# Expert 0's first 256 rows multiplied while the last batch is routed

## The chip, the cores and the metric

One Trainium2 chip, of which the kernel uses one core. The metric is the time of one execution in microseconds on the device. The kernel before was run three times: 780.51, 781.54 and 781.69 us, median 781.54. Less is better.

## The reference

```python
# q, k, v, alpha: (4, 8, 768, 48); 3072 tokens of 384 features, 8 experts of width 1024
for t in range(S):
    state = alpha[:, :, t, :, None] * state + np.einsum('bhd,bhe->bhde', k[:, :, t], v[:, :, t])
    y[:, :, t] = np.einsum('bhd,bhde->bhe', q[:, :, t], state)
...
expert_idx = np.argmax(logits, axis=1)            # logits: normed x times normed embeddings, by tau
gate_w = probs[np.arange(N), expert_idx]
for e in range(E):
    mask = expert_idx == e
    h = np.maximum(x[mask] @ w1[e], 0.0)
    out[mask] = gate_w[mask, None] * (h @ w2[e])
...
h = x @ w_in                                      # 384 -> 2048 -> 384 for every token
g = np.maximum(0.01 * h, h)
return (g @ w_out).astype(np.float32)
```

A gated linear attention over four batches gives 3072 tokens. Each token goes to the expert with the largest score (top 1); the expert's two layers are applied to it, and a dense pair of layers to the result. In the reference's inputs expert 0 has 309 tokens in the first three batches and 418 in all four; the largest expert has 426.

## The kernel before

The work has three stages. In the first, attention runs in 16 units (4 batches of 4 pairs of heads), and each finished batch is routed: scores, largest score, rank of the token within its expert, and then six indirect DMAs from GpSimd (`scatter`, L595) write the batch's 768 rows to `bucket`, a table in DRAM with 3072 rows for each expert. The rows carry the scale, the gate and the token's number behind the 384 features. The routing of a batch runs inside the next batch's attention; that of the last batch has nothing beside it.

In the second stage (from L800) the eight experts follow one another. Of each, exactly 432 rows (`CAP`) are computed, more than any expert has here: what is beyond its tokens was zeroed earlier by `zero_rows`, and a loop at the end (L1067) takes what is past 432, which is empty here. Every number is kept as a pair of f16 values (high and low), so a product takes three: high by high, high by low, low by high. The first layer (`up`) has 8 groups (f) of 3 x 3 products of 432 columns, the second (`down`) 3 groups (d) of 8 x 3; together 144 products. Expert 0's rows are fetched in four blocks, scaled on VectorE, turned on TensorE (`first_rows`, L853); the other experts' rows are scaled to f16 pairs on ScalarE and VectorE and turned by DMA (`block`, L875). Meanwhile the next expert's weights are fetched in 8 pieces of 384 KB (L892), into five stage buffers, and split into f16 pairs on ScalarE and VectorE (L897, L898), and a part of the last layers' 64-bit weights is converted on the way (`double`, L907).

In the third stage the dense pair of layers runs over blocks of 512 tokens.

In the first two stages the order of the instructions on each engine comes from a planner (`Plan`, L44): every operation is added with an engine, a cost, what it reads and writes, and a due time `at`. `order` takes at each step the operation that can start first, and among those within 0.15 us of it the one with the smallest `at`. The second plan's DMA is modelled at 230 KB/us. Each engine then executes in that order; on SyncE (SP), which issues most DMAs, it is also the order of the transfers' issue. In the first plan, fillers (`keep_busy`, L335) are put where TensorE would be idle. A tile of a later stage that takes the place of an earlier stage's memory waits for all that used it: for SBUF this includes the scatters, which read the batch's rows. PSUM has a pool of its own.

Between the plans stand the sum of the counts (L711 to L721), which gives `n_e`, and 56 fillers (L714). In the second plan `START` (L820) and `begin(e)` set the due times; `pieces_of(e)` lists expert e+1's pieces and the 64-bit pieces by due time, and L987 puts the first four ahead of expert 0's rows.

## Time and profile before

| | us |
|---|---|
| median of three runs | 781.54 |
| the profiled execution's own time | 780.79 |
| its span, first to last instruction | 779.2 |
| TensorE busy | 757.4 (97%) |
| VectorE busy | 452.4 (58%) |
| ScalarE busy | 341.0 (44%) |
| GpSimd busy | 98.9 (13%) |

TensorE's busy time counts the fillers as well: 172 of them in the trace, 53.2 us. A group of rows below is read as: start and length in us, engine, line, operation, out<-in, shapes, count, and in brackets the idle time of the engine before it with what ended it. PE is TensorE's product, PEld its load of weights, DVE VectorE, ACT ScalarE, POOL GpSimd, and SPq the issue of a DMA on SyncE. Start times count from the first instruction of the span.

### The profile page before, as it was taken

To read this page: it belongs to the slowest core of one execution; us is meant where nothing else is said; L and a number is where in the kernel's file an instruction comes from. 1 tells how busy PE (TensorE), PEld (TensorE's weight loads), DVE (VectorE), ACT (ScalarE), POOL (GpSimd) and SP (SyncE) were. 2 spreads that over 40 slices of the span, in tenths; PEclk is the share of its full clock that TensorE was granted. 3 is DMA by queue.
4 is the path that set the end of the run, shared out by engine and by line. 5 is a ranking of instruction groups with operands and counts; after the bars stand their busy time and mean duration, and the time that the engine had idled before them with its cause. 6 is when DMAs were issued, how large, how long until landed. Compare 5 with 4: busy or idle time off the path is not lost.

```text
span 779.2 us, 12948 instructions
## 1 busy us (share of the span) xinstructions
PE 757.4 (97%) x5109; PEld 426.8 (55%) x5109; DVE 452.4 (58%) x776; ACT 341.0 (44%) x673; POOL 98.9 (13%) x108
## 2 busy tenths in 40 slices
PE   8999999988999999999999999999999999999995
PEld 4777767644555555555544654554554564465462
DVE  8989999747688788878866126116306404503600
ACT  2343636416576676757635125215205404403500
POOL 6122624321010000000000110010010010010011
PEclk9999999999999999999999999999999999999998
DMA  8984945228998998787100000000000000000000
GB/s 301 349 257 133 294 140 191 93 96 208 198 226 218 225 247 171 212 229 222 42 3 1 20 21 1 11 31 0 11 21 11 1 31 11 1 21 21 1 21 23
DMA packets 58466, 84.08 MB, mean 108 GB/s; under 512 B 26648, under 2 KB 37664, under 8 KB 58400
## 3 DMA queue, kind: packets, MB, share of 16 engines
q1 hardware_dynamic: 54752, 73.66, 34.7%
q0 software_dynamic: 3648, 9.53, 3.2%
q8 instruction: 42, 0.69, 0.4%
q14 instruction: 24, 0.20, 0.1%
HBM read 66.80 MB, written 11.73 MB: 101 GB/s over the span
## 4 chain that ended last, share of the span: by engine, by line
issue 46%; PE 39%; DVE 5%; POOL 4%; DMA 3%; ACT 1%; SPq 0%; POOLq 0%; ACTq 0%
PE ps L965 4%; PE ps L964 4%; PE ps L963 4%; PE ps L940 4%; PE ps L939 4%; PE ps L938 4%; POOL out L797 3%; PE psc L396 2%; PE py L447 2%; PE py L415 2%; PE pfill L336 2%; DMA v<-in_v 1%; DVE rc L369 1%; PE ptr L475 1%; DVE am L401 1%
## 5 line engine op out<-in xcount | busy, mean ns | idle before, releaser
L780 DVE SCALAR_TENSOR_TENSOR g<-ps,r 128x512 f32<-128x512 f32 x96 | 65.7, 684 | 150.2 <-ACT r L779 150.2
L792 PE MATMUL ps<-woh,gh 128*128 128x384 f16 x384 | 125.2, 326 | 0.0
L793 PE MATMUL ps<-wol,gh 128*128 128x384 f16 x384 | 125.2, 326 | 0.0
L794 PE MATMUL ps<-woh,gl 128*128 128x384 f16 x384 | 125.2, 326 | 0.0
L774 PE MATMUL ps<-x2h,wih 128*128 128x512 f16 x288 | 109.1, 379 | 1.4 <-DVE x2l L970 1.4
L775 PE MATMUL ps<-x2l,wih 128*128 128x512 f16 x288 | 109.2, 379 | 0.0
L776 PE MATMUL ps<-x2h,wil 128*128 128x512 f16 x288 | 109.2, 379 | 0.0
L784 DVE TENSOR_TENSOR gl<-g,gh 128x512 f16<-128x512 f32 x96 | 66.4, 692 | 65.4 <-ACT gh L783 65.4
L783 ACT ACTIVATE gh<-g 128x512 f16<-128x512 f32 x96 | 60.4, 630 | 82.7 <-DVE g L780 82.6
L796 ACT ACTIVATE osb<-ps,ms 128x384 f32<-128x384 f32 x24 | 14.0, 582 | 159.3 <-PE ps L794 159.3
L797 POOL DMA_INDIRECT out<-osb,tki x24 | 23.7, 987 | 352.1 <-ACT osb L796 345.2
L938 PE MATMUL ps<-xt,w1h 128*128 128x432 f16 x192 | 66.4, 346 | 0.0
L939 PE MATMUL ps<-xt,w1h 128*128 128x432 f16 x192 | 66.4, 346 | 0.0
L940 PE MATMUL ps<-xt,w1l 128*128 128x432 f16 x192 | 66.4, 346 | 0.0
L963 PE MATMUL ps<-hh,w2h 128*128 128x432 f16 x192 | 66.4, 346 | 0.0
L964 PE MATMUL ps<-hl,w2h 128*128 128x432 f16 x192 | 66.4, 346 | 0.0
L965 PE MATMUL ps<-hh,w2l 128*128 128x432 f16 x192 | 66.4, 346 | 0.0
L779 ACT ACTIVATE r<-ps 128x512 f32<-128x512 f32 x96 | 56.0, 583 | 10.8 <-PE ps L776 10.8
L336 PE MATMUL pfill<-busy,ones 128*128 128x512 f16 x172 | 53.2, 411 | 2.1 <-POOL busy L189 2.1
L793 PEld LDWEIGHTS <-gh 128*128 128x128 f16 x384 | 37.6, 98 | 25.1
L792 PEld LDWEIGHTS <-gh 128*128 128x128 f16 x384 | 37.6, 98 | 25.1
L794 PEld LDWEIGHTS <-gl 128*128 128x128 f16 x384 | 37.6, 98 | 24.8
(198 smaller groups left out, 1131.6 us busy)
## 6 DMA issues: line engine op xcount, KB each, us to landing
wstage<-in_w SPq DMA_DIRECT2D x64, 384.0 KB, 5.7
a<-in_aT SPq DMA_DIRECT2D x16, 387.5 KB, 4.4
k<-in_kT SPq DMA_DIRECT2D x16, 384.0 KB, 6.2
q<-in_qT SPq DMA_DIRECT2D x16, 384.0 KB, 6.6
wstage<-in_w_in SPq DMA_DIRECT2D x16, 384.0 KB, 5.7
wstage<-in_w_out SPq DMA_DIRECT2D x16, 384.0 KB, 3.5
v<-in_v SPq DMA_DIRECT2D x8, 576.0 KB, 7.9
xg<-bucket SPq DMA_DIRECT2D x7, 582.0 KB, 7.2
```

Of the source, the lines that this page charges most:

```text
L774: nc.tensor.matmul(ps, wih[:, k, fs], xh[:, k], start=k == 0, stop=False)
L775: nc.tensor.matmul(ps, wih[:, k, fs], xl[:, k], start=False, stop=False)
L776: nc.tensor.matmul(ps, wil[:, k, fs], xh[:, k], start=False, stop=k == KD - 1)
L792: nc.tensor.matmul(ps, ghs[f][:, ts], woh[:, f], start=f == 0, stop=False)
L793: nc.tensor.matmul(ps, ghs[f][:, ts], wol[:, f], start=False, stop=False)
L794: nc.tensor.matmul(ps, gls[f][:, ts], woh[:, f], start=False, stop=f == NF2 - 1)
L938: nc.tensor.matmul(ps, w1h[:, f, k], xt[:, k], start=k == 0, stop=False)
L939: nc.tensor.matmul(ps, w1h[:, f, k], xt[:, KD + k], start=False, stop=False)
L940: nc.tensor.matmul(ps, w1l[:, f, k], xt[:, k], start=False, stop=k == KD - 1)
L963: nc.tensor.matmul(ps, w2h[:, f, cols], hh, start=f == 0, stop=False)
L964: nc.tensor.matmul(ps, w2h[:, f, cols], hl, start=False, stop=False)
L965: nc.tensor.matmul(ps, w2l[:, f, cols], hh, start=False, stop=f == NF1 - 1)
```

## The change

Expert 0 is split by rows: its first 256 (`E0`) and the other 176. When the third batch's rows are in the bucket, the first 256 rows of expert 0 are fetched within the first plan (`early_rows`), scaled on ScalarE, turned on TensorE and kept as f16 pairs (`xte`). The second plan has both layers of expert 0 for these 256 columns ahead of everything else, and for the other 176 columns after expert 0's last two blocks of rows. The hidden values (`hid`) and `xte` lie in a pool that is made ahead of the routing stage (`keep`); `xte` shares its place with the sign buffers of the 64-bit pieces, and the hidden values' tiles are used again in the last layers. The 56 fillers between the plans and the twelve of `first_rows` are gone. `START` is 5.5 and not 20. Six and not four pieces of weights stand ahead of the gathers; expert 1's rows are fetched in blocks and have an early due time. The token numbers and gates of expert 0 are copied from DRAM to DRAM. If expert 0 had fewer than 256 tokens in three batches (`few`), its first two blocks would be computed again in the loop for leftovers.

```diff
+E0 = 2 * P
...
+    seen, few = (const.tile([P, 1], F32, name=n) for n in ("seen", "few"))
+    keep = ctx.enter_context(tc.tile_pool(name="keep", bufs=1))
+    hid = [[keep.tile([P, BLK], F16, name=f"h{x}{f}") for f in range(NF1)] for x in "hl"]
+    shared = keep.tile([P, 2 * W64], F32, name="shared")
+    xte = shared.bitcast(F16).rearrange("p (k t) -> p k t", k=2 * KD)
...
+            if b == B - 2:
+                small(V, lambda: nc.vector.tensor_copy(seen, cnt[:, 0:1]), ["cnt"], ["seen"])
...
+        def early_rows():
+
+            u = (NU - 3) % 3
+            rows = (ta[u][:, :AUG], tq[u][:, :AUG])
+            scaled = (ta[u][:, AUG:AUG + D], tk[u][:, :D])
+            for n in range(E0 // P):
+                ts = slice(n * P, (n + 1) * P)
+                hi, lo = xte[:, :KD, ts], xte[:, KD:, ts]
+                held = ("a", "q")[n], u
+
+                def fetch(n=n, ts=ts):
+                    nc.sync.dma_start(rows[n], bucket[ts])
+
+                def turn(n=n):
+                    for k in range(KD):
+                        nc.tensor.transpose(ptr[n][:, k], scaled[n][:, k * P:(k + 1) * P], ident)
+
+                plan.add(Q_, 0.45, fetch, [("bucket", B - 2, c) for c in range(NC)], [held], size=(P * AUG * 4, 2.5))
+                plan.add(S_, 0.62, lambda n=n: nc.scalar.activation(scaled[n], rows[n][:, :D], AF.Copy, scale=rows[n][:, D:D + 1]), [held], [("early", n)] + [("k", u)] * n)
+                plan.add(T_, 0.45, turn, [("early", n)], [("tr", n)], pe=[f"t{n}"], flow=KD * P)
+                plan.add(S_, 0.47, lambda n=n, hi=hi: nc.scalar.activation(hi, ptr[n][:, :KD], AF.Copy), [("tr", n)], [("xte", n)], ps=[f"t{n}"])
+                plan.add(V, 0.56, lambda n=n, hi=hi, lo=lo: nc.vector.scalar_tensor_tensor(lo, ptr[n][:, :KD], 1.0, hi, op0=ALU.mult, op1=ALU.subtract),
+                         [("tr", n), ("xte", n)], [("xtl", n)], ps=[f"t{n}"])
...
-            z0 = 2 * P
+            z0 = 0 if e == 0 else 2 * P
 
             def go():
-                nc.sync.dma_start(bucket[e * NT + z0:e * NT + z0 + P], zero)
-                nc.sync.dma_start(bucket[e * NT + z0 + P:e * NT + CAP], zero[:CAP - z0 - P])
+                for o in range(z0, CAP, P):
+                    nc.sync.dma_start(bucket[e * NT + o:e * NT + min(o + P, CAP)], zero[:min(P, CAP - o)])
...
+            plan.at = NU + 1.7
+            early_rows()
...
-            nc.vector.tensor_copy(tc16, cnt)
-            tot = pkv[:, 0:E]
+            nc.vector.tensor_copy(tc16[:, :E], cnt)
+            nc.vector.tensor_copy(tc16[:, E:], seen)
+            tot = pkv[:, 0:E + 1]
             nc.tensor.matmul(tot, ones16, tc16, start=True, stop=True)
-            for _ in range(56):
-                keep_busy("f")
-            nc.vector.tensor_tensor(n_e, tot, row0, op=ALU.subtract)
+            nc.vector.tensor_scalar(few, tot[:, E:], float(E0), None, op0=ALU.is_lt)
+            nc.vector.tensor_tensor(n_e, tot[:, :E], row0, op=ALU.subtract)
...
-        START, TURN = 20.0, 26.4
+        START, TURN = 5.5, 26.4
...
-            if e == 0:
-                for n in range(NB):
-                    plan.add(Q_, 0.45, lambda n=n: block(n), ["bucket"], [("xg", 0), ("row", n)], size=(P * AUG * 4, 2.5), at=0.0)
+            if e < 2:
+                for n in range(0 if e else E0 // P, NB):
+                    plan.add(Q_, 0.45, lambda n=n: block(n), ["bucket"], [("xg", e), ("row", e, n)], size=(P * AUG * 4, 2.5), at=float(e))
             else:
-                plan.add(Q_, 0.9, most, ["bucket"], [("xg", e % 2)] + ([("row", n) for n in range(NB)] if e == 2 else []), size=CAP * AUG * 4, at=begin(e - 2) + 8 if e > 1 else 20.0)
+                plan.add(Q_, 0.9, most, ["bucket"], [("xg", e % 2)] + [("row", e % 2, n) for n in range(NB)], size=CAP * AUG * 4, at=begin(e - 2) + 8,
+                         after=[("xt", 1, NB - 1, 0)] if e == 2 else ())
...
+                if e == 0:
+                    nc.gpsimd.dma_start(meta[:CAP], bucket[:CAP, D + 1:D + 3])
+                    return
...
-                for _ in range(6 if n == NB - 1 else 2):
-                    nc.tensor.matmul(ps2[3], ones16, busy[:, :CAP], start=True, stop=True)
...
-            at = begin(e - 1) + 1.0 + 4.0 * n
-            plan.add(S_, 0.62, lambda: nc.scalar.activation(xs[:, 0], x, AF.Copy, scale=r), [("xg", e % 2)], [("xs", g, 0)], at=at)
+            at = begin(e - 1) + 1.0 + 4.0 * n if e > 1 else n - 15.0
...
-        def up(e, f):
-            xt, (w1h, w1l), ps = xts[e % 2], shaped(sets[e % 2])[:2], ps1[f % 4]
-            hh, hl = hid[0][f], hid[1][f]
-            at = begin(e) + 1.65 * f - 12.0
+        def step(n):
+
+            return max(0.1, n * 0.1828 / CAP)
+
+        def up(e, f, xt, at, cols, early=False):
+            (w1h, w1l), n = shaped(sets[e % 2])[:2], cols.stop - cols.start
+            ps, hh, hl = ps1[f % 4][:, :n], hid[0][f][:, cols], hid[1][f][:, cols]
 
             def go():
                 for k in range(KD):
@@ -939,9 +977,11 @@
                     nc.tensor.matmul(ps, w1h[:, f, k], xt[:, KD + k], start=False, stop=False)
                     nc.tensor.matmul(ps, w1l[:, f, k], xt[:, k], start=False, stop=k == KD - 1)
 
-            plan.add(T_, 1.65, go, [("w", e % 2, 0, f // 2, i) for i in range(2)] + [("xt", e % 2, n, i) for n in range(NB) for i in range(2)], [("ps1", f % 4)], at=at)
-            plan.add(S_, 0.52, lambda: nc.scalar.activation(hh, ps, AF.Relu), [("ps1", f % 4)], [("h", f, 0)], at=at)
-            plan.add(V, 0.605, lambda: nc.vector.scalar_tensor_tensor(hl, ps, 0.0, hh, op0=ALU.max, op1=ALU.subtract), [("ps1", f % 4), ("h", f, 0)], [("h", f, 1)], at=at)
+            rows = [("sg", i) for i in range(2)] if early else [("xt", e % 2, b, i) for b in range(cols.start // P, NB) for i in range(2)]
+            key = ("h", f, early)
+            plan.add(T_, 9 * step(n), go, [("w", e % 2, 0, f // 2, i) for i in range(2)] + rows, [("ps1", f % 4)], at=at)
+            plan.add(S_, 0.16 + n / 1200, lambda: nc.scalar.activation(hh, ps, AF.Relu), [("ps1", f % 4)], [(*key, 0)], at=at)
+            plan.add(V, 0.155 + n / 960, lambda: nc.vector.scalar_tensor_tensor(hl, ps, 0.0, hh, op0=ALU.max, op1=ALU.subtract), [("ps1", f % 4), (*key, 0)], [(*key, 1)], at=at)
...
+            for f in range(NF1):
+                up(0, f, xte, f - 40.0, slice(0, E0), True)
+            for d in range(KD):
+                down(0, d, d - 30.0, slice(0, E0), True)
             mine = pieces_of(0)
-            add(mine[:4])
+            add(mine[:6])
             gather(0)
             gather(1)
-            add(mine[4:])
-            for n in range(NB):
+            add(mine[6:])
+            for n in range(E0 // P, NB):
                 first_rows(n)
...
+                cols = slice(0 if e else E0, CAP)
                 for f in range(NF1):
-                    up(e, f)
+                    up(e, f, xts[e % 2][:, :, cols], begin(e) + 1.65 * f - 12.0, cols)
...
+            E1 = E + 1
+            spare = shared[:, :2 * OVB * E1].rearrange("p (m e) -> p m e", e=E1)
...
```

`down` is split in the same manner as `up`; expert 0's results go to a fixed place (columns 0 to 431), so the reading of its offset falls away. The block that computes the leftovers' list (L1019) has nine entries instead of eight and some eight small VectorE instructions more. Expert 0's rows are zeroed from row 0.

## Rows read from the trace of the kernel before

**Rows 1.** The page's head: the span of the profiled execution.
```profile
span 779.2 us, 12948 instructions
```

**Rows 2.** Busy time by stage: stretch, its length, engines, granted clock, DMA share, GB/s.
```profile
core 0: us, PE busy (x) PEld busy (x) DVE busy (x) ACT busy (x) POOL busy (x), PEclk, DMA share, GB/s
...
173.00:178.00 5.00, 4.09 (x19) 1.67 (x17) 3.68 (x6) 3.33 (x6) 0.00 (x0) 1.00 0.82 225
178.00:184.10 6.10, 3.88 (x25) 2.40 (x26) 4.57 (x11) 2.27 (x5) 0.83 (x1) 1.00 0.98 340
184.10:210.40 26.30, 26.30 (x146) 14.11 (x145) 19.11 (x35) 16.67 (x31) 3.15 (x5) 1.00 0.81 161
210.40:236.80 26.40, 26.40 (x146) 14.13 (x145) 20.71 (x35) 16.76 (x31) 2.07 (x3) 1.00 1.01 242
```

**Rows 3.** Time line of PE, from routing's end into expert 0's second layer.
```profile
163.14 0.17 PE L713 MATMUL pkv<-c,ones 128*128 128x8 f16 x1 [1.43 <-DVE c L711]
...
165.63 11.46 PE L336 MATMUL pfill<-busy,ones 128*128 128x512 f16 x48
179.78 0.52 PE L860 MATMUL ps<-ident,xs 128*128 128x128 f32 x3 [2.69 <-issue]
...
184.06 0.35 PE L938 MATMUL ps<-xt,w1h 128*128 128x432 f16 x1
...
197.20 0.35 PE L963 MATMUL ps<-hh,w2h 128*128 128x432 f16 x1
```

**Rows 4.** Loads of weights: time line in routing; by line (ns min/median/max) for the experts.
```profile
161.38 0.20 PEld L575 LDWEIGHTS <-ones 128*128 128x128 f16 x5 [0.82 <-issue]
...
L938 PEld LDWEIGHTS <-w1h x192: 97/98/98, 183.9 to 380.4; 128*128 128x128 f16 x192
```

**Rows 5.** Time lines of ACT, DVE, POOL and SP in the same stretch.
```profile
161.23 0.24 ACT L582 ACTIVATE ex<-lg 128x48 f32<-128x48 f32 x1 [1.61 <-DVE lg L581]
172.64 0.84 ACT L897 ACTIVATE w1h<-wstage 128x768 f16<-128x768 f32 x1 [11.17 <-DMA bucket<-xb,slot]
...
163.34 0.17 DVE L716 TENSOR_TENSOR n_e<-pkv,row 128x8 f32<-128x8 f32 x1 [0.26 <-PE pkv L713]
173.52 0.96 DVE L898 SCALAR_TENSOR_TENSOR w1l<-wstage,w1h 128x768 f16<-128x768 f32 x1 [8.44 <-ACT w1h L897]
178.87 1.03 DVE L864 TENSOR_SCALAR xs<-xg 128x384 f32<-128x384 f32 x2
...
163.30 0.97 POOL L596 DMA_INDIRECT bucket<-xb,slot  x1 [7.83 <-issue]
169.67 0.96 POOL L596 DMA_INDIRECT bucket<-xb,slot  x1 [0.30 <-issue]
...
172.57 1.75 SPq L829 DMA_DIRECT2D xg<-bucket  x4
```

**Rows 6.** Landing: third batch's scatters; expert 0's gathers; fetches of 175 to 180.
```profile
L596 POOL DMA_INDIRECT bucket<-xb,slot x6: 965/967/1172, 147.9 to 154.5; - x6
DMA to landing us min/median/max: 2.6/2.7/5.0
...
DMA to landing us min/median/max: 2.5/3.2/3.9
...
DMA to landing us min/median/max: 5.9/6.6/7.7
```

**Rows 7.** Busy time and granted clock in two short stretches (columns as in rows 2).
```profile
165.00:167.00 2.00, 2.00 (x6) 0.69 (x5) 0.08 (x1) 0.00 (x0) 1.52 (x2) 0.50 0.45 164
177.00:179.70 2.70, 0.10 (x1) 0.00 (x0) 2.70 (x5) 0.77 (x2) 0.83 (x1) 1.00 0.99 290
```

**Rows 8.** Last conversions for experts 1 and 4 (DVE); expert 4's second layer begins (PE).
```profile
210.19 0.96 DVE L898 SCALAR_TENSOR_TENSOR w2l<-wstage,w2h 128x768 f16<-128x768 f32 x1 [2.34 <-ACT w2h L897]
299.74 0.94 DVE L898 SCALAR_TENSOR_TENSOR w2l<-wstage,w2h 128x768 f16<-128x768 f32 x1
...
302.32 0.35 PE L963 MATMUL ps<-hh,w2h 128*128 128x432 f16 x1
```

More of the change, by code (lines that the diff above doesn't have):

```diff
@@ L536, in part_squares @@
             x, w = txb[b % 3][:, :, 2 * h * HD:2 * (h + n) * HD], late[:, :, :2 * n * HD]
-            small(S_, lambda: nc.scalar.activation(w, x, AF.Square), [("xb", b % 3, u, g) for u in range(h, h + n) for g in range(2)], ["late"], 0.2 + 0.48 * n)
+            small(S_, lambda: nc.scalar.activation(w, x, AF.Square), [("xb", b % 3, u, g) for u in range(h, h + n) for g in range(2)], ["late", ("junk", 0), ("junk", 1)], 0.2 + 0.48 * n)
             small(V, lambda: nc.vector.tensor_reduce(tsm[b % 2][:, row], w, AX.X, ALU.add), ["late"], [("part", h)], 0.1 + 0.6 * n)
@@ L780, in second_in @@
             nc.vector.scalar_tensor_tensor(g, ps, 2.0 ** -6, r, op0=ALU.mult, op1=ALU.max)
-            gh = gp.tile([P, n], F16, name=f"gh{f}")
-            gl = gp.tile([P, n], F16, name=f"gl{f}")
+            gh, gl = (hid[i][f][:, :n] if f < NF1 else gp.tile([P, n], F16, name=f"g{i}{f}") for i in range(2))
             nc.scalar.activation(gh, g, AF.Copy)
@@ L967, in down @@
             for f in range(NF1):
-                plan.add(T_, 0.55, lambda f=f: go(f), [("w", e % 2, 1, f // 2, i) for i in range(2)] + [("h", f, i) for i in range(2)], [("ps2", b)], at=at + 0.55 * f)
-            plan.add(S_, 0.52, lambda: nc.scalar.activation(x2h[:, d, ds(offset[0], CAP)], ps, AF.Copy, scale=2.0 ** -8), [("ps2", b), ("place", 0)], [("x2", e, d)], at=at)
-            plan.add(V, 0.605, lambda: nc.vector.scalar_tensor_tensor(x2l[:, d, ds(offset[1], CAP)], ps, 2.0 ** -8, x2h[:, d, ds(offset[1], CAP)], op0=ALU.mult, op1=ALU.subtract),
-                     [("ps2", b), ("x2", e, d), ("place", 1)], [("x2l", e, d)], at=at)
+                plan.add(T_, 3 * step(n), lambda f=f: go(f), [("w", e % 2, 1, f // 2, i) for i in range(2)] + [("h", f, early, i) for i in range(2)], [("ps2", b)], at=at + 0.05 * f)
@@ new lines, in place @@
+            def place(i):
+                return cols if e == 0 else ds(offset[i], CAP)
+            where = [] if e == 0 else [("place", i) for i in range(2)]
+            plan.add(S_, 0.16 + n / 1200, lambda: nc.scalar.activation(x2h[:, d, place(0)], ps, AF.Copy, scale=2.0 ** -8), [("ps2", b)] + where[:1], [("x2", e, d)], at=at)
+            plan.add(V, 0.155 + n / 960, lambda: nc.vector.scalar_tensor_tensor(x2l[:, d, place(1)], ps, 2.0 ** -8, x2h[:, d, place(1)], op0=ALU.mult, op1=ALU.subtract),
+                     [("ps2", b), ("x2", e, d)] + where[1:], [("x2l", e, d)], at=at)
```

92 lines of the change are left out of this document (49 added, 43 removed).

## The prediction

> **What bounds the kernel now.** I read the page's head first (the span, [rows 1]), then the time line of TensorE around the end of routing, then the time lines of the other engines in the same stretch, then the busy time by stage, and last the conversions of the weights. TensorE is busy nearly everywhere, so busy time says little; what matters is which of its work is the kernel's. From the last product of routing at 163.14 to the first product of expert 0 at 184.06 it computes nothing that is kept: 57 fillers, of which one row has 48, then a gap of 2.69 us, then turns of rows with more fillers [rows 3]. These 20.9 us are a chain on other engines: scores of the last batch, six scatters on POOL from 163.30, the last at 169.67, their landing, the gathers on SP at 172.57, and behind ACT's first conversion (172.64, after 11.17 us of waiting for the scatters) a queue of conversions, until VectorE scales expert 0's first rows at 178.87 [rows 5]. Behind the chain stand eight experts of even length. Expert 0's first layer is 72 products of 432 columns in 184.06 to 197.20 [rows 3], 0.1825 us each. An expert has 144, so 26.3 us, and TensorE is full in that stage [rows 2]. Only two things shorten the kernel here: an earlier first product of the rest, or less work behind it. The change aims at the second.
>
> **What is removed and added on TensorE.** Expert 0's 144 products of 432 columns (26.3 us) become 144 of 256 columns ahead of the release and 144 of 176 behind it. At a granted clock of 1.00 (2.4 GHz) 432 columns are 180.0 ns of the 182.5, so I price a product at columns/2.4 GHz + 2.5 ns: 109.2 ns for 256, 15.7 us for the early block. For 176 that gives 75.8 ns, 10.9 us, if nothing but columns counts. The other end is the load of the weights: each product has one, 97 to 98 ns long [rows 4]; if loads of different weights ran one after the other the rest would take 144 x 97.5 = 14.0 us. But in the routing's small products five such loads of 128x128 f16 fit into 0.20 us, so they start about 25 ns apart and overlap [rows 4]. I take 80 ns, 11.5 us, near the low end, and keep both.
>
> The row says that a load does not hold up the next product for its length. The Trainium skill ("TensorE: Matmul & The Clock Gate", section "LDWEIGHTS (loading the stationary operand)") speaks against the change here: it prices a load at columns/1.2 in ns, 107 ns for 128, and by that the rest would be 15.4 us, 3.9 us more than I take; the same page's "Back-to-back issue gap" has about 81 ns for a sustained pair at 128 columns, which would make it 11.7 us at least. No run before shows distinct weights with so few columns.
>
> **When the early block runs.** It needs the scatters of the third batch, its own rows, and PSUM. The third batch's last scatter starts at 154.5 and these land in 2.6 to 5.0 us [rows 6], so SP can fetch at 157.3 to 159.5; two fetches of 128 rows land 2.5 to 3.9 us later [rows 6], by about 161 to 163.4. They read the bucket that the last batch's scatters write, so POOL's scatter, at 163.30 [rows 5], waits for them: nothing at the near end, 0.1 us at the far one; I take nothing. The plan's ready times put the early scaling on ACT behind the last batch's Exp (161.23 [rows 5]), and the early low halves on VectorE behind its routing chain; so nothing of routing is queued behind a fetch except that scatter. Scaling, turning and splitting two blocks cost by the planner 0.62 + 0.45 + 0.47 + 0.56 us, two of them overlapped: done at about 164.3. The counts wait behind them on VectorE (n_e moves from 163.34 to about 165.2), but nobody needs n_e before the experts. The first early product waits for n_e, since that is the last read of the routing's PSUM: about 165.4. The clock is at 0.50 (1.2 GHz) in 165 to 167 [rows 7], after the gap that ends with the sum of the counts [rows 3]; I let that stand for 2 us of early block, +1.0 us. So the block ends at 165.4 + 15.7 + 1.0 = 182.1, under the wait. Its evacuations are hidden except in one place: ACT has the first conversion of expert 1's weights between the sixth and the seventh Relu by the planner's times, and that conversion waits for the release (172.64). The sixth group's Relu is due at about 172.4, so this costs nothing at half clock, up to 1 us without; both ends stay under the wait.
>
> **When the rest starts.** Before the gathers SP now has six fetches instead of four. The early fetch holds the first four back from the 140s to about 159, which hides behind the release. The fifth waits for the release, and the sixth takes stage buffer 0, freed by ACT's first conversion and VectorE's part of it: 172.64 + 0.84 + 0.96 = 174.5. So the gathers leave at about 175.0 instead of 172.57 and land, behind a fetch, in 2.5 to 6.6 us [rows 6], at 178 to 181. Two more pieces (some 3 us of VectorE) stand ahead of the scaling, but two blocks instead of four follow it. Before, the way from the first scaling to the first product was 184.06 - 178.87 = 5.2 us for four blocks. With scaling at 180 and 4 us for two blocks and the conversions between, I get 184.5; bounds 183 (conversions hide) and 186 (the sixth piece lands late and ACT waits for it). So the start stays where it was, within the bounds.
>
> **The sum up to expert 1.** 184.5 + 11.5 = 196.0, against 184.06 + 26.3 = 210.4: 14.4 us. This is where it can be given back: expert 1's rows and every later weight are wanted 14.4 us earlier.
>
> **The supply.** Expert 1's last piece of weights is converted at 210.19 + 0.96 = 211.2 [rows 8], wanted at 210.4 + 13.1 + 3.3 (the seventh of eight steps of its second layer) = 226.8: 15.6 us to spare. Expert 4's is ready at 299.74 + 0.94 = 300.7, wanted at 302.32 + 3.3 = 305.6 [rows 8]: 4.9 us. Three experts' pieces took 89.5 us, where TensorE takes 78.9. With demand 14.4 us earlier, 9.5 us must be found or TensorE waits. In 173 to 210.4 the DMA engines were idle for 0.18 x 5 + 0.02 x 6.1 + 0.19 x 26.3 = 6.0 us [rows 2]; two gather blocks fewer, and two fetches some 3 us earlier, give 3 to 4 more. After 210.4 hardly anything is left (share 1.01). So 9 to 10 us against 9.5: I take 1.5 us of waiting, spread over experts 1 to 4, ends 0 and 9.5.
>
> **Small edits.** Zeroing 256 more rows of expert 0 is 0.4 MB in the attention stage; put_meta(0) goes from DRAM to DRAM and frees the row buffer earlier; one copy (seen) in batch 2: nothing, between engines that wait for others there. Some eight more small VectorE operations stand ahead of the last layer's evacuations, 0.17 us each like n_e [rows 5], 1.4 us; the last layer has four PSUM banks of work in hand: 0 to 1.4, I take 0.2. In the reference's inputs expert 0 has 309 tokens in the first three batches and 418 in all, no expert over 426: the early rows are full, and the loop for leftovers stays empty.
>
> Sum: -14.4 + 1.5 + 0.2 = -12.7 us against the profiled execution, 780.79 with a span of 779.2 [rows 1]: 768.1. The median of the three runs is 781.54, 0.75 higher, so I say 769.0. Best within the bounds: 183, 10.9, no waiting: 16.5 us, 764.8 to 765.0. Worst: 186, 14.0, 3 us of waiting: 7.4 us, 774.
>
> **Rivals.** (1) Weight loads set the pace of the narrow products: 14.0 us instead of 11.5, and some 0.5 us less of waiting for supply: 771. For it: loads 97 ns long; against it: starts 25 ns apart [rows 4]. 0.15. (2) The supply cannot be pulled forward, since conversions stand in fixed orders between evacuations and DMA is full: only the 4.9 us that expert 4 has to spare are gained, 776.6. For it: share 1.01 in 210 to 237 [rows 2]; against it: 0.81 before that, and that the orders move with TensorE. 0.15. (3) The change doesn't do what it says: the early products wait for the release of the routing stage's memory, as ACT's conversion does (172.64): the block ends at 172.6 + 15.7 = 188.3, the rest starts at 188.8, 4.3 us of the gain are lost and about 1 of waiting saved: 772.3. Against it: they write only PSUM and tiles made outside that stage. 0.07. (4) Slower: without the 57 fillers and the twelve of the turns the clock stays at 1.2 GHz over both narrow blocks. Then the early block ends at 165.4 + 31.2 = 196.6 and the rest takes 144 x 147 = 21.2 us: 218.2 against 210.4, +7.8 us, 789. It decides once some 29 us of this stretch run at half, since each costs half a microsecond of 14.4. Against it: the 2.7 us without products at 177 to 179.7 left the clock at 1.00 [rows 7], and the early block is dense. 0.05.
>
> **How the numbers follow.** Forecast 0.57, rivals 0.15, 0.15, 0.07, 0.05, and 0.01 for a net near nothing. The range 764.5 to 776 holds the forecast's bounds, rivals 1 and 3 and the near half of 2; left out are the rest of 2, 4 and the forecast's tail, under 0.2. A change under 0.2% (1.6 us) could not be told from none. Faster 0.94, same 0.01, slower 0.05.
>
> **What would show it.** In the trace after: products of 256 columns from about 165 and before the last scatter lands; their spacing 109 ns; the rest at 183 to 186; the spacing of the 176-column products, 76 to 98 ns, decides rival 1; expert 1 at 195 to 200; TensorE's waits between there and 300, none before, sum to 0 to 3 us (rival 2: 9); granted clock 0.50 for 2 us or for 29. The forecast is wrong if the gathers leave later than 176, if TensorE waits more than 4 us for weights, or if the scatters move from 163.3.

## The result and the profile after

The changed kernel takes 771.76 us (median of four runs, 769.78 to 773.2), the kernel before 781.56 beside it: ratio 0.9876, 95% interval 0.9852 to 0.99, 9.8 us less. The forecast was 769.0 with a range of 764.5 to 776, so the time is inside, 2.8 us above the forecast. The profiled execution has a span of 769.7 against 779.2 [rows 1], 9.5 us less; the forecast's sum was 12.7. What follows finds the 3.2 us between these.

TensorE's busy time by stage in the trace after (stretch, its length, busy time and products, granted clock, share of the DMA engines, GB/s); these answer to [rows 2, 7]:

```profile
166.20:183.60 17.40, 17.37 (x144) 0.90 0.51 160
183.60:186.05 2.45, 1.05 (x9) 1.00 0.99 325
186.05:197.20 11.15, 11.14 (x144) 1.00 1.00 219
197.20:381.90 184.70, 184.33 (x1009) 1.00 0.84 206
381.90:384.76 2.86, 0.17 (x1) 1.00 0.00 0
384.76:388.20 3.44, 3.44 (x9) 0.50 0.00 0
```

The first row is the early block, 144 products with part of them at half clock. The second is the step to the rest of expert 0: turns and a wait. The third is the rest, the fourth experts 1 to 7. The last two are new: an idle step ahead of the third stage, and behind it nine products at half clock. The same two stretches of the kernel before:

```profile
394.30:395.84 1.54, 0.17 (x2) 1.00 0.11 2
395.84:399.30 3.46, 3.46 (x17) 1.00 0.45 9
```

There the step is 1.3 us shorter, and 17 products pass in the time of nine.

TensorE's time line in the trace after, around the early block, the rest and expert 1; it answers to [rows 3]:

```profile
162.35 0.18 PE L580 MATMUL psc<-oh,before 128*128 128x48 f16 x1 [0.55 <-DVE oh L576]
...
165.65 0.17 PE L749 MATMUL pkv<-c,ones 128*128 128x9 f16 x1 [1.44 <-DVE c L747]
166.23 0.30 PE L976 MATMUL ps<-shared,w1h 128*128 128x256 f16 x1 [0.41 <-DVE ohs L753]
...
183.50 0.27 PE L1004 MATMUL ps<-hh,w2l 128*128 128x256 f16 x1
183.61 0.81 PE L896 MATMUL ps<-ident,xs 128*128 128x128 f32 x6
185.36 0.24 PE L976 MATMUL ps<-xt,w1h 128*128 128x176 f16 x1 [0.94 <-ACT xt L901]
186.05 0.24 PE L977 MATMUL ps<-xt,w1h 128*128 128x176 f16 x1 [0.46 <-DVE xt L902]
...
196.98 0.24 PE L1004 MATMUL ps<-hh,w2l 128*128 128x176 f16 x1
197.06 0.35 PE L976 MATMUL ps<-xt,w1h 128*128 128x432 f16 x1
```

The lines of the kernel before for the first and the last of these:

```profile
161.37 0.18 PE L573 MATMUL psc<-oh,before 128*128 128x48 f16 x1 [0.55 <-DVE oh L569]
...
210.34 0.35 PE L938 MATMUL ps<-xt,w1h 128*128 128x432 f16 x1
```

Expert 1 begins at 197.06, 13.28 us earlier than the 210.34 of before. What matters is what stands between the early block's last product (183.50) and the rest: the turns follow on TensorE at once, at 183.61, with the same spacing as in e2_gathers_first below, where the rows were scaled before the block ended, so they did not wait for rows; then TensorE waits for ScalarE's copy (0.94) and VectorE's low part (0.46).

TensorE's waits from 199 to 400 us in the trace after (who waited for whom: us in total, times, longest):

```profile
PE ps L809 <- DVE x2l L1014: 2.7, 1, 2.7
PE ps L1004 <- DVE w2l L933: 0.2, 1, 0.2
```

The step to the third stage is the longest wait; waits for converted weights show with 0.2 us. By the starts of the products, experts 1 to 7 take 184.67 us from the first to the last of their 1008 products, 183.78 before, so 0.89 us are lost there, in three small gaps between 259 and 271.

The balance is then: -13.28 at expert 1, +0.89 in the experts, +1.32 for the step (3.04 us from product to product, 1.72 before), and +1.7 for 3.4 us at half clock: -9.4 of the 9.5.

### The profile page after: what moved, and what is told of

It is laid out like the page before. It is cut to its first block, busy times and chain, and to the rows that moved or that the text cites. A ratio compares the mean times of both kernels' runs of the same rounds, so it can differ in the third digit from the quotient of the medians.

```text
span 769.7 us, 13141 instructions
## 1 busy us (share of the span) xinstructions
PE 745.8 (97%) x5190; PEld 432.1 (56%) x5190; DVE 453.6 (59%) x795; ACT 342.2 (44%) x686; POOL 97.7 (13%) x108
## 4 chain that ended last, share of the span: by engine, by line
issue 47%; PE 34%; DVE 6%; DMA 5%; POOL 3%; ACT 2%; SPq 1%; POOLq 0%; ACTq 0%; DVEq 0%
PE ps L977 4%; PE ps L976 4%; PE ps L978 4%; PE ps L1004 3%; PE ps L1003 3%; PE ps L1002 3%; POOL out L831 3%; PE psc L403 3%; PE py L454 2%; PE py L422 2%; DMA wstage<-in_w_in 2%; PE pfill L343 2%; DMA v<-in_v 1%; DMA wstage<-in_w 1%; PE ptr L482 1%
## 5 line engine op out<-in xcount | busy, mean ns | idle before, releaser
L1004 PE MATMUL ps<-hh,w2l 128*128 128x432 f16 (+2 forms) x216 | 70.2, 326 | 0.3 <-DVE w2l L933 0.2
L1002 PE MATMUL ps<-hh,w2h 128*128 128x432 f16 (+2 forms) x216 | 70.2, 326 | 0.0
L1003 PE MATMUL ps<-hl,w2h 128*128 128x432 f16 (+2 forms) x216 | 70.2, 326 | 0.0
L976 PE MATMUL ps<-xt,w1h 128*128 128x432 f16 (+1 forms) x192 | 63.6, 333 | 0.9 <-ACT xt L901 0.9
L977 PE MATMUL ps<-xt,w1h 128*128 128x432 f16 (+1 forms) x192 | 63.6, 333 | 0.5 <-DVE xt L902 0.5
L978 PE MATMUL ps<-xt,w1l 128*128 128x432 f16 (+1 forms) x192 | 63.6, 333 | 0.1
L828 PE MATMUL ps<-woh,hl 128*128 128x384 f16 x192 | 62.6, 326 | 0.0
L826 PE MATMUL ps<-woh,hh 128*128 128x384 f16 x192 | 62.6, 326 | 0.0
L827 PE MATMUL ps<-wol,hh 128*128 128x384 f16 x192 | 62.6, 326 | 0.0
L828 PE MATMUL ps<-woh,g 128*128 128x384 f16 x192 | 62.6, 326 | 0.0
L827 PE MATMUL ps<-wol,g 128*128 128x384 f16 x192 | 62.6, 326 | 0.0
L826 PE MATMUL ps<-woh,g 128*128 128x384 f16 x192 | 62.6, 326 | 0.0
```

The source lines that it names most:

```text
L826: nc.tensor.matmul(ps, ghs[f][:, ts], woh[:, f], start=f == 0, stop=False)
L827: nc.tensor.matmul(ps, ghs[f][:, ts], wol[:, f], start=False, stop=False)
L828: nc.tensor.matmul(ps, gls[f][:, ts], woh[:, f], start=False, stop=f == NF2 - 1)
L976: nc.tensor.matmul(ps, w1h[:, f, k], xt[:, k], start=k == 0, stop=False)
L977: nc.tensor.matmul(ps, w1h[:, f, k], xt[:, KD + k], start=False, stop=False)
L978: nc.tensor.matmul(ps, w1l[:, f, k], xt[:, k], start=False, stop=k == KD - 1)
```

## The experiments

The experiments ran on other chips, where the kernel before takes 786 to 788 us. So each time is given as a ratio to the kernel before run beside it; these have intervals of some +-0.2%, 1.5 to 2 us, too wide for most single steps. Where each stage begins is therefore read from the trace, counted from the last batch's rank products (the products with `before` at 161.37 and 162.35 above, which both kernels have and which the change does not touch). All times are in us; "lost" is the time from expert 1's first product to expert 7's last, less the 183.78 that they take without a wait, and "step" is from there to the third stage's first product.

| kernel | ratio to before (95%) | rank products at | expert 1 begins after | lost in experts 1 to 7 | step | half clock behind it |
|---|---|---|---|---|---|---|
| before | 1 | 161.37 | 48.97 | 0 | 1.72 | no |
| c1_before, another chip | one run | 166.37 | 50.73 | 0 | 1.72 | no |
| after | 0.9876 (0.9852 to 0.99) | 162.35 | 34.71 | 0.89 | 3.04 | yes |
| c0_after, another chip | 0.9863 (0.9838 to 0.9888) | 166.32 | 34.58 | 3.76 | 3.12 | yes |
| e1_no_zero | 0.9883 (0.986 to 0.9906) | 166.59 | 34.56 | 1.67 | 3.23 | no |
| e2_gathers_first | 0.987 (0.9852 to 0.9888) | 169.30 | 35.69 | 0 | 3.32 | yes |
| e3_past_later | 0.9872 (0.9854 to 0.9891) | 169.67 | 34.71 | 0.63 | 1.62 | no |
| e5_half_block | 0.9972 (0.9955 to 0.9989) | 167.80 | 44.84 | 0 | 2.34 | no |
| e8_turns | 0.9872 (0.9852 to 0.9892) | 166.19 | 33.13 | 3.18 | 3.12 | no |
| e9_turns_past | 0.9837 (0.9814 to 0.986) | 167.89 | 33.14 | 5.54 | 1.62 | no |
| e10_fill | 0.9842 (0.9818 to 0.9865) | 170.31 | 33.96 | 4.36 | 1.62 | no |
| e11_meta | 0.985 (0.9832 to 0.9868) | 166.19 | 35.71 | 0 | 3.14 | yes |
| e12_best | 0.979 (0.9766 to 0.9814) | 166.14 | 32.96 | 0.27 | 1.62 | no |

**Half the early block.** Is it the columns multiplied early that make the gain?

```diff
-E0 = 2 * P
+E0 = P
-    xte = shared.bitcast(F16).rearrange("p (k t) -> p k t", k=2 * KD)
+    xte = shared.bitcast(F16)[:, :2 * KD * E0].rearrange("p (k t) -> p k t", k=2 * KD)
```

> Edit to the changed kernel: 128 instead of 256 rows of expert 0 are taken early, 304 instead of 176 columns are left to the rest. Theory A: the gain is the number of columns multiplied ahead of the gathers. 144 early products of 128 columns take 8.0 us by columns (55.8 ns each; up to 10.9 if weight loads set a floor near 75 ns), end near 176, TensorE then waits some 10 us for the gathers, the rest takes 144 x 129.2 ns = 18.6 us from 186.5 (and 1.7 more if the clock falls in the wait), so expert 1 starts at 205 to 207 instead of 197.2. Of these 8 to 10 us the waits that the changed kernel has later (0.9 us for weights, 1.3 us and a half clock of 1.7 us at the third stage) come back: 776 to 780, taken 778. Theory B: most of the gain is the earlier supply and order, not the columns: 772 to 774.

Ratio 0.9972, 779.4 us on the scale of the first runs, and expert 1 44.84 us behind the rank products instead of 34.71. TensorE's time line at the end of the early block of 128 columns:

```profile
184.93 0.22 PE L1004 MATMUL ps<-hh,w2l 128*128 128x128 f16 x1
189.01 2.16 PE L896 MATMUL ps<-ident,xs 128*128 128x128 f32 x9 [3.87 <-DVE xs L898]
```

With half the columns, TensorE waits 3.87 us for the gathered rows, which it does not do in the changed kernel, and nothing is lost behind expert 1. Of the 10.1 us, 7.7 are the columns: 144 x (129.2 - 75.8) ns, the spacings of 304 and of 176 columns in the two traces. Besides, the rest begins 1.1 us later and its first 3.9 us are at half clock. The theory of the columns holds. Where nothing holds them up and the clock is full, products of 128 columns with different weights follow one another every 55.8 ns: no floor near 75. The early block as a whole took 13.7 us, since half clock and waits for the hidden values fell into it too.

**The zeros.** Routing ends 1.0 us later in the trace after; the forecast had put the zeroing of 256 more rows at nothing.

```diff
-            z0 = 0 if e == 0 else 2 * P
+            z0 = 2 * P
```

> Edit to the changed kernel: expert 0's rows 0 to 255 of the bucket are not written with zeros in the first units (as in the kernel before; the other experts' rows and expert 0's rows from 256 on still are). Theory A: these 0.4 MB of extra zeros are what made the routing stage end 1.0 us later (last batch's rank products at 162.35 instead of 161.37; the wait on the v load on TensorE 2.1 us instead of 1.1). Then without them the rank products are back at 161.4 (161.1 to 161.7), the first early product at 165.3 instead of 166.23, the gathers at 175.8 instead of 176.75, expert 1 at 196.2 instead of 197.2, and the time is 771.8 - 1.0 = 770.8 us. Theory B: the 1.0 us has another cause (the early blocks' place in the planned order, other loads): the rank products stay at 162.3 and the time at 771.8.

The rank products stand at 166.59, and the kernel before has them at 166.37 on another chip (c1_before) where the changed kernel has 166.32 (c0_after), so nothing shows this difference to be a property of the change; the wait for the first v load, in the first 14 us and ahead of all zeros, is 2.7 us without these zeros, 2.1 with them in the first profile. Theory A falls.

> The kernel before itself, one more profile, for where its routing stage ends on the chip of the experiments. Theory A: the rank products' time is scatter of chip and execution and not of the change: here they stand between 165 and 169 as in the eight profiles of edited kernels (165.8 to 170.3), instead of 161.37. Theory B: the change made the stage later: they stand at 161 to 162 here too. Either way the stretches behind them: expert 1 begins 49.0 us behind the rank products and the third stage 234.5, as in the first profile.

Theory A holds for the rank products. The other two stretches were 50.73 and 236.2 us, 1.7 more than expected: on that chip TensorE's wait for expert 0's rows took 4.8 us from product to turn, and the clock fell behind it. So single stretches scatter by 1 to 2 us, and a step smaller than that is read from several profiles or not at all.

**Half clock or ScalarE.** e1_no_zero shows something else. It runs the early block at a granted clock of 1.00, and the block still ends as late as at half clock. ScalarE's time line and TensorE's longest wait in the block:

```profile
172.92 0.66 ACT L983 ACTIVATE hh<-ps 128x256 f16<-128x256 f32 x2 [3.90 <-PE ps L978]
177.03 1.21 ACT L983 ACTIVATE hh<-ps 128x256 f16<-128x256 f32 x4 [3.44 <-PE ps L978]
```

```profile
PE ps L976 <- DVE hl L984: 1.4, 1, 1.4
```

The third Relu starts at 177.03 although its products began at 172.43 and ended a microsecond later; four Relus then run in a burst, and the seventh group waits 1.4 us for a free bank. The first Relu waits as well, until 172.92: ahead of it on ScalarE stands a read of `offi`, which VectorE ends at 172.0. What holds the third Relu is not in the trace. It starts 10.4 to 10.5 us behind the rank products in seven profiles (e1_no_zero, e3_past_later, c0_after, e8_turns, e9_turns_past, e11_meta and e12_best), and 10.4 to 10.5 behind them start the second in e2_gathers_first and e10_fill and the fourth in e5_half_block; in the first profile the third starts at 8.7, where it follows its products. So something that keeps time with the routing seems to hold ScalarE there; what it is stays open.

**The gathers.** The forecast had the rest start when the gathered rows were ready.

```diff
-            add(mine[:6])
+            add(mine[:5])
             gather(0)
             gather(1)
-            add(mine[6:])
+            add(mine[5:])
...
-    after=[("xg", 1)] if len(fetched) > 6 else ()
+    after=[("xg", 1)] if len(fetched) > 5 else ()
```

> Edit to the changed kernel: five instead of six weight fetches ahead of the six gathers in SyncE's queue, so that no gather stands behind a fetch that waits for the first conversion. Theory A: the gathers leave at 173.7 instead of 176.75 and land before 180; the rest products then wait only for the early block and start at 184.4 instead of 186.05, and expert 1 at 195.6 instead of 197.2. If the weights of experts 2 and 3 have slack, the time falls by these 1.6 us to 770.2. Theory B: the supply of weights is already at its limit (products waited for converted weights for 0.9 us in all between 259 and 271 us): the gain at expert 1 is given back there (these waits grow to 2 to 2.5 us) and the time stays at 771.8. Theory C: the rest is not held by the gathers: expert 1 stays at 197.2.

The gathers left 11.6 us behind the rank products instead of 14.4, and expert 1 began no earlier (35.69; the early block began 1.4 us later there, behind a stretch at half clock); in the experts nothing is lost in this profile. TensorE's and VectorE's time lines of e2_gathers_first:

```profile
191.27 0.27 PE L1004 MATMUL ps<-hh,w2l 128*128 128x256 f16 x1
191.38 0.81 PE L896 MATMUL ps<-ident,xs 128*128 128x128 f32 x6
193.13 0.24 PE L976 MATMUL ps<-xt,w1h 128*128 128x176 f16 x1 [0.94 <-ACT xt L901]
```

```profile
189.98 0.41 DVE L898 TENSOR_SCALAR xs<-xg 128x384 f32<-128x384 f32 x1
190.78 0.41 DVE L898 TENSOR_SCALAR xs<-xg 48x384 f32<-48x384 f32 x1
```

From the block's last product to the rest it is 1.86 us, as in the changed kernel (183.50 to 185.36). Theory C: the rest is held by the early block, and by turns, copy and low part, which the order on TensorE puts behind it. So, with the fetches in this order, the turns were moved, one ahead of the last 24 early products and one among them:

```diff
-            plan.add("WAIT", 10.8, lambda: None, [], ["bucket"])
+            plan.add("WAIT", 8.0, lambda: None, [], ["bucket"])
...
-                down(0, d, d - 30.0, slice(0, E0), True)
+                down(0, d, d - (30.0 if d < KD - 1 else 10.0), slice(0, E0), True)
```

> Edit to the changed kernel: five fetches ahead of the gathers as in e2_gathers_first, the planner's wait for the scatters 8.0 instead of 10.8, and the last 24 early products of the second layer put behind the turns of the rest's rows, so that the turns and their copies to xt run beside those products. Theory A: what holds the rest is the early block itself and the chain turns, copy, low part behind it (1.86 us from the block's last product to the rest in steady products, the same in five profiles, with the gathers early or late). Then the rest starts within 0.3 us of the early block's last product, expert 1 some 1.6 us earlier against the rank products, and the time is 1.6 us under the changed kernel's, or less by what the waits for converted weights grow (0.9 us in the first profile, at most 2.5). Theory B: the gathered rows land too late for the turns there: TensorE waits ahead of the turns and the time is the changed kernel's or up to 1.5 us more.

TensorE's time line of e8_turns:

```profile
184.83 0.49 PE L896 MATMUL ps<-ident,xs 128*128 128x128 f32 x3
186.23 0.38 PE L896 MATMUL ps<-ident,xs 48*128 48x48 f32 x3
...
188.09 0.27 PE L1004 MATMUL ps<-hh,w2l 128*128 128x256 f16 x1
188.20 0.24 PE L976 MATMUL ps<-xt,w1h 128*128 128x176 f16 x1
```

The rest follows the block at the next product; expert 1 begins at 33.13, 1.45 us earlier than in c0_after. That part of theory A is shown. In the time nothing of it is seen (0.9872 against 0.9863, each +-0.002). In this profile 3.18 us are lost in the experts, but in that of c0_after 3.76; where the other executions lost the gain no trace shows.

> The changed kernel itself, for its time beside the next three on one chip. From the first profile: rest of expert 0 starts 23.0 us behind the last batch's rank products, the step from the last product of expert 7 to the first of the third stage is 3.0 us. Theory A: the rank products' own time (162.3 there, 166.6 to 169.7 in the four experiments before) is scatter of the routing stage and not of the change, so ratio to the kernel before 0.985 to 0.990. Theory B: the change itself makes the routing stage later by 1 us or more: the rank products of this profile stand over 163 again.

Theory A by the ratio; the rank products' 166.3, which theory B also names, are those of c1_before too. This profile of the changed kernel loses 3.76 us in the experts, where the first lost 0.89.

**The third stage.** On VectorE the last x2l, for which the third stage's first product waits, ran at 384.10 in the trace after, though ScalarE's half was done at 382.64:

```profile
382.39 0.45 DVE L1094 TENSOR_TENSOR shared<-shared,c 128x288 f32<-128x288 f32 x1
...
383.74 0.45 DVE L1100 TENSOR_TENSOR ee<-ee,c 128x288 f32<-128x288 f32 x1
384.10 0.60 DVE L1014 SCALAR_TENSOR_TENSOR x2l<-ps,x2h 128x432 f32 x1
```

L1092 to L1100 belong to `past_static`, which works out the list of leftovers. In the kernel before, one operation of it (0.36 us) stood ahead of the last x2l:

```profile
394.90 0.36 DVE L1025 TENSOR_TENSOR ob<-ob,n_e 128x192 f32<-128x192 f32 x1 [3.60 <-POOL ob L1022]
395.18 0.60 DVE L970 SCALAR_TENSOR_TENSOR x2l<-ps,x2h 128x432 f32 x1
```

```diff
-            nc.vector.tensor_copy(cb[:, 0:1], nb_e[:, 0:1])
+            nc.vector.scalar_tensor_tensor(cb[:, 0:1], x2l[:, KD - 1, 0:1], 0.0, nb_e[:, 0:1], op0=ALU.mult, op1=ALU.add)
```

> Edit to the changed kernel: the first link of the chain that works out the rows past expert capacity reads one column of x2l's last part times zero, so that the chain runs on VectorE behind the last x2l instead of ahead of it. Theory A: the third stage starts late in the changed kernel because 1.5 us of this chain stand ahead of the last x2l on VectorE, and the idle of 3.0 us is what drops the clock to half for 3.4 us. Then the step from the last product of expert 7 to the first of the third stage is 1.6 us instead of 3.04, the clock stays at 1.00 there, and the time is 771.8 - 1.4 - 1.7 = 768.7 us. Theory A2: the step gets shorter but the clock falls all the same: 770.4. Theory B: the last weight pieces of the second layer (the last low part ends at 382.5) hold the third stage: the step stays near 3 us and the time at 771.8.

TensorE's and VectorE's time lines of e3_past_later:

```profile
388.79 0.35 PE L1004 MATMUL ps<-hh,w2l 128*128 128x432 f16 x1
390.40 0.38 PE L809 MATMUL ps<-x2h,wih 128*128 128x512 f16 x1 [1.27 <-DVE x2l L1014]
```

```profile
389.74 0.61 DVE L1014 SCALAR_TENSOR_TENSOR x2l<-ps,x2h 128x432 f32 x1 [1.69 <-ACT x2h L1013]
390.38 0.16 DVE L1081 SCALAR_TENSOR_TENSOR c<-x2l,c 128x1 f32<-128x1 f16 x1
```

The step is 1.62 us and the third stage begins at full clock. From expert 7's last product to the end of the span it is 384.9 us here and 385.1 in e9_turns_past and e10_fill, which have the same edit; without it the first profile has 388.0, e1_no_zero 386.7, e2_gathers_first 389.5, c0_after 388.1, e8_turns 386.6; the kernel before 385.1. The shorter step of theory A is shown by the trace. That the clock stays up because of it rests on a count over all profiles: it fell behind none of the seven steps up to 2.34 us and behind four of the six over 3. The time (0.9872 against 0.9863) does not show the gain; this profile's routing stage ends 3.4 us later than c0_after's, and the other executions have no trace.

> Edit: e8_turns and e3_past_later together. Theory A: the step to the third stage is 1.6 us instead of 3.0 to 3.3 and the clock does not fall there, on top of the 1.6 us of e8_turns: 3 us (clock full in the other profile) to 4.7 us (clock at half there) under the changed kernel, ratio to the kernel before 0.981 to 0.984. Theory B: what is gained ahead of expert 1 comes back as waits for converted weights, so only the third stage's 1.4 to 3.1 us are left.

Ratio 0.9837, under c0_after's 0.9863 but with overlapping intervals, and the step is 1.62. In the experts 5.54 us are lost, more than in any other kernel, part of it at half clock behind one wait of 2.3 us for expert 3's weights:

```profile
PE ps L976 <- ACT w1h L932: 2.3, 1, 2.3
```

The ratio fits both theories; the trace speaks for theory B in the rest's share: the earlier expert 1 is, the more TensorE waits for weights. The mean loss is 1.7 us in the four profiles that begin expert 1 at 34.6 to 34.7, 4.4 in the three that begin at 33.1 to 34.0, and nothing in the two that begin at 35.7 and later (e2_gathers_first, e5_half_block).

**Fillers ahead of the early block.**

```diff
+            for _ in range(6):
+                keep_busy("f")
             tc16 = tc16[0]
...
             nc.tensor.matmul(tot, ones16, tc16, start=True, stop=True)
+            for _ in range(2):
+                keep_busy("f")
```

> Edit: e9_turns_past, and filler products on TensorE in the two waits ahead of the early block (six between the early turns and the matmul of the totals, two behind it). Theory A: the early block's first products run at half clock because TensorE idles for 2.2 us just before them; with the fillers the granted clock stays at 1.00 from the early turns on and the block takes 15.8 us instead of 17.3, so 1.5 us less time. Theory B: the block's 17.3 us are set by the Relus' and conversions' waits on ScalarE (in e1_no_zero it took 17.2 us at full clock): no gain from the fillers. Theory C: the fillers themselves run at half clock and put off the totals by up to 1.5 us: slower than e9_turns_past by that.

Granted clock ahead of the block (the 0.50 of the first line), and TensorE's time line:

```profile
172.00:174.00 2.00, 2.00 (x10) 0.50 0.18 70
```

```profile
173.51 1.89 PE L343 MATMUL pfill<-busy,ones 128*128 128x512 f16 x6
175.24 0.17 PE L751 MATMUL pkv<-c,ones 128*128 128x9 f16 x1
```

Here the clock had fallen during routing, before the fillers, so they ran part of their time at half and put the totals off by 1.6 us (4.93 us behind the rank products, 3.30 in e9_turns_past); the block itself then ran at full clock, and took 17.2 us against 18.1 in e9_turns_past, 0.9 less and not the 1.5 of theory A. Expert 1 begins 0.8 us later than in e9_turns_past: theory C, at half its price. Whether fillers would have kept the clock in the first profile is not settled.

**What holds the weights.** The forecast took the DMA engines as the limit of the supply. Waits of TensorE (199 to 400 us) and of SyncE's queue (192 to 285 us) in c0_after:

```profile
PE ps L1004 <- DVE w2l L933: 1.4, 3, 0.7
PE ps L978 <- DVE w1l L933: 0.5, 1, 0.5
PE ps L976 <- DVE wil L955: 0.3, 1, 0.3
```

```profile
SPq L861 <- DMA meta<-xg: 21.7, 4, 6.4
```

SyncE, which issues every fetch of weights, stands 21.7 us at four gathers: each overwrites xg, from which a small DMA (`put_meta`, 8 bytes a row) is still reading; the fetches of the next weights are queued behind. One of the four on SyncE's time line, the wait between the two parts of a gather and the fetches (L927) behind it:

```profile
214.34 0.53 SPq L864 DMA_DIRECT2D xg<-bucket  x1
219.61 0.34 SPq L861 DMA_DIRECT2D xg<-bucket  x1
220.05 0.84 SPq L927 DMA_DIRECT2D wstage<-in_w  x2
```

In the kernel before these waits were 9.4 us, in three.

```diff
-                if e == 0:
-                    nc.gpsimd.dma_start(meta[:CAP], bucket[:CAP, D + 1:D + 3])
-                    return
-                so = nc.gpsimd.value_load(offi[0:1, e:e + 1], min_val=0, max_val=NT)
-                nc.gpsimd.dma_start(meta[ds(so, NF * P)].rearrange("(n p) c -> p n c", p=P), xg[:, :NF, D + 1:D + 3])
...
+                so = nc.gpsimd.value_load(offi[0:1, e:e + 1], min_val=0, max_val=NT) if e else 0
+                nc.gpsimd.dma_start(meta[ds(so, CAP)] if e else meta[:CAP], bucket[e * NT:e * NT + CAP, D + 1:D + 3])
```

> Edit to the changed kernel: the 8-byte records of each expert's rows (meta) are copied from the bucket in DRAM for every expert, as the change already does for expert 0, and no longer from the gathered rows in xg, so that the gather for expert e+2 needs not wait in SyncE's queue until that small copy has landed (19.3 us of such waits between 192 and 285 us in the first profile of the changed kernel, 21.7 in c0_after, each with the weight fetches of the next expert queued behind it). Theory A: these waits in SyncE's queue are what makes converted weights late for experts 1 to 3: the waits of TensorE for weights (0.9 us in the first profile, 3.7 in c0_after) go to under 0.5 us and the time falls by 1 to 3.5 us, ratio to the kernel before 0.982 to 0.985. Theory B: the DMA engines themselves are full there (share of busy time 0.95 to 1.1 from 197 to 276 us): SyncE's waits shift to other releasers, the waits of TensorE stay at 1 to 4 us, ratio 0.986 to 0.988.

TensorE's waits from 199 to 400 us in e11_meta:

```profile
PE ps L809 <- DVE x2l L1009: 2.8, 1, 2.8
```

All waits for weights are gone. But they are gone in e2_gathers_first too, which has three such waits in SyncE's queue (7.9 us) and begins expert 1 at 35.69, as late as the 35.71 here (behind three short waits in the rest). So this run alone does not tell the queue from a later expert 1; the run with both, below, does. What speaks against full DMA engines is their idle time in c0_after. The stretch from 226 to 256 us, c0_after and then e11_meta, with the share of the DMA engines and GB/s at the end:

```profile
226.00:256.00 30.00, 29.48 (x162) 1.00 0.80 170
226.00:256.00 30.00, 30.00 (x166) 1.00 0.89 240
```

With the waits in SyncE's queue the engines by this share stood idle for a fifth of the stretch, ahead of most of the waits for weights; without them they moved 240 GB/s and not 170. The ratio, 0.985, is at the edge of what theory A expected.

> Edit: e9_turns_past and e11_meta together. Theory A (SyncE's waits hold the weights): the 1.6 us of the earlier rest and the 1.4 to 3.1 us at the third stage both stay in the time: 3 to 6 us under the changed kernel, ratio to the kernel before 0.978 to 0.982. Theory B (the DMA engines are full): the rest's gain comes back as waits for weights, ratio as in e9_turns_past, 0.9837 +- 0.002.

TensorE's waits from 199 to 400 us in e12_best, all of them:

```profile
PE ps L809 <- DVE x2l L1009: 1.3, 1, 1.3
```

Ratio 0.979 (0.9766 to 0.9814), 16.5 us under the kernel before; its interval lies wholly under that of c0_after and under that of e11_meta, which ran on the same chip as this one. Theory A. Expert 1 begins at 32.96, earlier than in any other kernel, and 0.27 us are lost behind it, where e8_turns, e9_turns_past and e10_fill lost 3.18 to 5.54 with the copies from xg: the edit to these copies ends the waits for weights. The planner's order on SyncE moves by a few places with it, so that it is the queue, and not that order, rests on the vanished waits there. The step is 1.62 us and the clock stays up.

Not all of the gain is of this kind. From the last product to the end of the span it is 8.7 us in e11_meta and e12_best and 9.8 to 10.0 in the other profiles: GpSimd's closing DRAIN (a wait at the program's end, L1175 and L1180) is 4.8 us in e11_meta and 5.4 in c0_after. GpSimd issues 8 instead of 15 small copies with this edit; that this shortens the end is not shown. So about 1.2 us of both gains belong to the program's end and to no wait for weights.

## Why the prediction was right or wrong, point by point

**What bounded the kernel, and the columns.** Right. The 20.9 us at the end of routing took up the early block, and halving the block's columns put expert 1 off by 10.1 us, 7.7 of them by the columns (e5_half_block).

**The price of a product.** Right: 109.1 ns for 256 columns, 75.8 for 176, as columns/2.4 GHz + 2.5 ns gives. The rest took 11.0 us (186.05 to 197.06); I had taken 11.5, away from the row's own value and towards the loads, for no need. Rival 1 is refuted. The Trainium skill ("TensorE: Matmul & The Clock Gate", section "LDWEIGHTS (loading the stationary operand)") prices a load of 128 columns at 107 ns, which is its length, near the 97 to 98 ns of [rows 4]; that this sets the spacing of the products was my reading of it, and at 75.8 ns it does not. The same page's "Back-to-back issue gap" has about 81 ns for a sustained pair at 128 columns; with a load for each product it was 55.8 ns here (e5_half_block).

**The early block.** It ran before the scatters' landing, so rival 3 falls. It started at 166.23 and not 165.4, with routing 1.0 us later, a difference that nothing ties to the change. The first scatter moved with it, from 163.30 to 164.28, 1.93 us behind the rank products in both traces; I had named its moving as a sign against me, but without the routing's own scatter in mind. The block's clock was at half for 3.4 us and not 2, so it took 17.4 us instead of 16.7 and ended at 183.6 instead of 182.1. No more of the two narrow blocks was at half clock there, so rival 4 falls. On other chips the block ends as late at full clock, with TensorE waiting for hidden values that ScalarE begins late (e1_no_zero); the step that said "up to 1 us without" half clock was too small there (1.4 us of waiting).

**The start of the rest.** Here the mechanism was wrong. I let the gathers set it: 175.0, rows, scaling, 184.5. The gathers left at 176.75, later than the 176 that I had named as proof against me, and yet they set nothing: with the gathers 2.8 us earlier the step was the same (e2_gathers_first). What I left out is TensorE's own order: turns stand behind the block's last product, and the copies behind the turns, 1.86 us to the first product and 2.55 to steady ones. The number came out within its bounds (186.05 against 183 to 186) only because both ways were equally long.

**The supply.** 1.5 us of waiting forecast, 0.89 found, 0.6 to 3.8 in the other profiles of that order (e1_no_zero, e3_past_later, c0_after); rival 2's 9 us are refuted. The reason given, DMA engines without idle time, was wrong: from 226 to 256 us they were busy for 0.80 in c0_after. By e12_best it was the copies out of xg, and with them the gathers that SyncE's queue held for them.

**The last layer.** The step that failed. I took 0.2 us (0 to 1.4) for more VectorE work ahead of the last layer's evacuations and said that four banks of work were in hand. That stands within the last layer, not at its start: the first product of the third stage waits for the very last x2l, and with the change the list of leftovers is worked out ahead of that instruction: its first operation, on GpSimd, runs at 369.06 in the trace after and at 394.55, behind the last expert's products, in the trace before. 1.3 us of step were found, within the bound; what the bound lacked is the 1.7 us of half clock behind the longer step.

So of the 3.2 us between sum and trace, 1.1 come from expert 1's start (half clock, the chain of turns, routing, less the cheaper rest), -0.6 from the supply, and 2.8 from the third stage's start; 0.1 is left over. Two slips in the working change none of this: the best case is 780.79 - 16.5 = 764.3 and not 764.8, and rival 4's rest ends at 217.8 and not 218.2.

## What to carry to other kernels

When work is put into a wait, look for what follows it in program order on the same engine: the wait was also the cover of the turns, copies and small lists behind it, and each of them comes to the front when the cover goes. An in-order queue that issues the bulk loads must not hold a transfer that waits for a small, slow one; free its source another way. And price the idle steps at later stage borders too, since behind a step that grew from 1.7 to 3 us the clock fell in four of six profiles.

## What was not expected of the hardware

The clock fell to 0.50 behind the step to the third stage in four of six profiles with a step of 3.04 to 3.32 us (first profile, e2_gathers_first, c0_after, e11_meta; not e1_no_zero, e8_turns), and in none of seven with 1.62 to 2.34 us. The same kernel's trace can thus differ by 1.7 us at one place. The end of the routing stage, with the same work, lay between 161.4 and 170.3 us, half clock for some time between 156 and 174 us being part of it in all profiles of other chips. And products with a new 128x128 f16 weight each ran at the pace of their columns down to 128 columns: 55.8 ns (e5_half_block).
